# One mask operation for eight heads, and a new order of all five queues, in a fused attention and gated-MLP kernel

## The chip, the cores and the metric

The kernel runs on one core of a Trainium2 chip. The metric is the device time of one execution in microseconds (us), median of the runs shown. A core has five engines with a queue of instructions each, worked off in order: TensorE (PE: matmuls; PEld its weight loads), VectorE (DVE), ScalarE (ACT), GpSimd (POOL) and SyncE (SP), whose queue here issues nearly all DMA transfers. An engine waits for another only where an instruction waits for a semaphore.

## The reference: what is computed

One block with adaptive layer norm: sliding-window attention (16 heads of 28 columns, window 256), then a gated MLP whose gate mixes over the sequence. S = 2048, D = 448, bf16.

```python
mod = (_silu(c) @ w_mod).reshape(1, 6, 1, -1)
sa, ca, ga, sb, cb, gb = (mod[:, i] for i in range(6))
h = _layernorm(x) * (1 + ca) + sa
# attention: scores of query i and key k only where 0 <= i - k < 256
x = x + ga * (softmax(mask(q @ k.T * Dh ** -0.5)) @ v) @ wo
h = _layernorm(x) * (1 + cb) + sb
z = _gelu(h @ w_in)                       # 2048 x 1792
z1 = z[..., :896]; z2 = _layernorm(z[..., 896:])
g = w_sp @ z2 + b_sp                      # 2048 x 2048 times 2048 x 896
x = x + gb * ((z1 * g) @ w_out)
```

## The kernel before, in words

Work is listed once, as a graph: each call of `Sched.add` makes an `Op` with its possible engines, its dependencies, and the buffer slots that it takes. `Sched.order` (L155) does not plan anything. It reads a string, `PLAN`, written out by hand or by a program, of which each word is one operation: a letter for the engine (p TensorE, a ScalarE, d VectorE, t GpSimd, s SyncE), the operation's number, and the slots of its buffers. So the plan decides the engine (where an operation has a choice), the order in each queue, and the buffers; semaphore waits follow from these.

The stages, by the names that the profile shows:

- Loads. SP issues x in blocks (`load_x0` L408 for the first two pairs of tiles, `load_x` L398 for 512 rows each), w_mod and w_qkv in pieces (`load4` L404, some of them on ACT), `wv` and `wo` and the rest of w_mod (`wmodB`) through `load2` (L393), and `w_in` in three rows of 128 partitions and two halves (L432, L434). Transposed copies (`turn`, L465) go through SP as well: `hT<-xn` turns a normed tile, `hT<-o_sb` an attention output, `wspA` and `wspB` the 2048 x 2048 mixing matrix.
- First norm, per 128-row tile: statistics on VectorE (`stats`, L628, L630), a power on POOL (L632), the norm itself (L643, L650, with L648 for the negated mean), then for all but the first four tiles a transpose by DMA and a modulation of `hT` (L731).
- Queries, keys and values (TensorE L762, L796, L820, L840), evicted by ScalarE or VectorE (L771 and L772, L832 and L833, L844 and L845). L593 makes the two gates from `wmodB`, evicted as `gg_sb` (L596); L535 makes the second modulation from it.
- Attention, a loop over 16 query tiles `j` and two halves of 8 heads. A tile sees three key blocks: the far one and the near one are partly masked, the middle one is whole. Because the window's far edge and near edge together fill exactly one block, the two partly masked blocks are folded into one: L955 makes scores of a half into four PSUM banks of 512 columns, ScalarE takes the exponential of all 2048 columns at once into `PW` (L911), and VectorE multiplies the folded edges with a 0/1 mask into `PT` (L974), one operation for each of the two pairs `k` of key and query groups, 1024 columns each. L966 adds a leftover of the middle block. L1002 multiplies the probabilities with the values (`Vaug`, which also sums each row); it takes the edges from `PT` and the middle from `PW`. L1016 and L1018 normalise, SP turns the result, L1028 multiplies with wo, L1032 adds it to x.
- Second norm (same lines as the first, with the turn into `hT`), modulation L1053; then z2 (L1122, evicted with gelu by L1129, normed by L1134), z1 (L1143, L1151), the mixing product (L1167, 448 matmuls of 512 columns), its bias (L1171), the gate (L1174), the output product (L1186), the sum with x (L1196) and the store (L1201).

Where each edge lies in a bank is set by three numbers for even and odd tiles: `at_m0` and `at_hm` for the parts of the middle block, `at_f` for the two folded edges. A head's columns in `PW` take `PWT` = 576.

Of the kernel before, what the change touches and what calls it, by code (L numbers as in the profile page):

```python
# [12 lines left out]
d24 d22 p50.1 p59.3 p51.2 p58.0 p60.1 p62.0 a0 a3 a5 a7 a9 d23 d25 d26 d27 p40.1 p68.2 p74.3 p64.1 p52.0 p67.2  # L13
p53.3 p76.0 p49.3 p70.0 s1 s2 s4 d113 s6 s10 s8 a41 p45.0 p46 p47.1 p48 p73.2 p75.1 p63.2 t30 t31 t32 t35 t36
t33 d111 d114 t34 d112 t115 t37 a103 t29 t105 t38 d117.3 d116.2 p125.7 d86 d85 p128.0 p78.0 a129 a130 d106
d126 d127 d120 d121 d118 d119 a107 p83.1 p80.0 p81.1 p79.2 p77.0 p55.3 p72.2 p71.0 s12 d183 d181 p65.1 t104
p54.0 p149.1 p84.2 p140.5 p141 p150 a151 p82.1 p57.2 a142 t109 t110 t108 p137.7 p138 a139 p66.2 t122 d124.2
d123.0 p134.3 p131.6 p69.3 p56.0 p146.0 p147 p61.2 a132 d177 d184 d135 a136 s13 d243 d179 d178 d182 d180 t28
t185 t191 t187 t189 d245 d44 d241 d186.3 s11 p143.7 p370.0 a133 p164.1 p171.6 p172 d244 p165 d166 a148 p152.0
p144 d145 d173 d247 p153 d154 a371.0 p376.0 p155.1 p156 d157 a42 a377.4 p394.0 a395.1 a396 a170 t39 d380 d372  # L20
d246 d167 d374 p158.7 p159 a160 s15 p93.1 p94 d95 d248 d87 d88 d242 d397 p96.0 p97 d98 d378 s193 t188.1 s194
t190.2 s195 t192.0 s196 d197 d200 p401.0 a402.5 p174.1 p175 a176 p161.7 p162 p373.0 p89.0 p90 d91 d198 d92
a403 a43 p421.0 a422.6.0 t249 t253 d404 t251 t199 p375 p379 p381 d406 d382 d399 t252.2 d163 p217.0 p218 a219
a169 p210.1 p211 d212 p429.0 a430.0 p201.0 p202 a203 d168 p204.1 p205 a206 s14 d309 d383.2 p398.0 p400 p448.0
a449.2.1 s16 d426 s831 s258 t254.1 s259 d250.0 d255 d425 d432 d311 s384 s257 t256.3 s260 t100 t99 t261 t102
t262 t264 p226.0 p423.0 a424 p207.1 p227 p405 p208 d228 d305 p407 d408 d409.1 d306 s410 d101 d310 d431 a209
d215 d453 p456.0 p229.0 a457.1 d459 d214 d458 d452 p220.1 p221 p230 a231 p427.0 p428 s833 p475.0 p433 p434
d435 p223.0 p224 d225 d312 p450.0 a222 p232.1 d436.2 s437 d213 a476.3.2 d480 p483.0 d307 p233 d234 p235.0 p236
a451 a216 p477.0 p454.0 p455 a484.0 p501.0 d485 d486 d308 s21 s17 s834 p460 p461 d462 d479 d463.0 s464 a237
t263 p385.0 p386 d387 p411.1 p412 a478 p503.0 d413 t313 a502.6.0 p528.0 a504 d388 d505 d389 p481.0 p482 p487  # L30
p488 p271.0 p530.0 d489 d490.1 a529.2.1 d533 d506 d532 p272 a273 p509.0 a510.5 p268.1 p274.0 p275 d276 p269
d270 p507.0 p508 a531 p555.0 a556.3.2 p281.0 p265.1 p266 a267 d512 p282 p557.0 a558 a283 d511 p513 t317 t318.1
s323 t319 t320.2 s324 d314.0 s321 t315 t316.3 s322 t328 d279 d414 d560 p536.0 a537.1 p438.1 p439 d440 d280
p514 d515 d516.0 p287.0 p288 a289 p290.1 p291 a292 p563.0 a564.5 p238.0 p239 d278 p293.1 p534.0 p294 p535
p582.0 a240 p465.0 p466 d441 d442 d538 d415 d277 s20 s491 s830 s517 t390 d539 d391.2 t392 s393 a295 a583.4.0
d559 p540 p541 p284.1 p584.0 p285 a286 p590.0 a591.2 d566 d467 p299.0 p300 a301 d542 d543.1 p561.0 p562 d586
d565 d468 p567 p568 p608.0 t416 t327 t325 d326 d587 p518.1 p335.0 p519 d569 d570.0 p588.0 a585 p589 p336 d593
d469 d520 a609.3.1 p616.0 d592 d521 d417 d522 t523 t470 t418.0 t524 p338.1 p339 a337 s544 p545.0 p546 s18 p594
p595 a617.5 p635.0 a636.6.2 p610.0 a611 d340 p492.1 p493 d547 p296.0 p297 a298 t471 d596 d597.2 d612 p614.0
d613 s835 s571 s598 d494 t419 s420 d640 d548 d619 d549 d618 d495 t443 t444 t445.1 t446 s447 p662.0 a663.0.0  # L40
d667 p615 p332.0 p333 a334 p329.1 p330 a331 d639 d343 t472.2 d473 s474 p643.0 a644.1 p599.0 p600 p637.0 a638
p345.1 p346 p620 a347 d601 d602 d344 d645 d666 d342 p670.0 a671.2 p621 p664.0 d622 d496 p348.0 p349 a350
p357.1 p358 t550 t551 t552.0 t804 d623.2 s624 p689.0 d646 d673 d525.2 p302.0 p303 d304 d672 s19 p641.0 p642
p647 p648 d649 d805 t553 d650.0 s651 t526 s527 t497 t806 t803 d498.1 t499 s500 a690.5.1 p697.0 a359 p351.1
p352 d341 d353 a665 d693 d603 a698.1 d700 d694 p668.0 p363.0 p364 a365 p715.0 a716.3.2 p669 p674 p675 p691.0
a692 d699 d676 d677.2 s678 p354.1 p355 p572.0 a356 d720 d719 p723.0 a724.2 p717.0 a718 p573 d574 d575 p695.0
p696 p701 d725 p702 d703 d704.0 s705 s554 d576 p652.0 p742.0 a743.0.1 p366.1 p367 a368 d726 p653 d654 t577
d578 t579.2 d746 d655 p721.0 p722 p727 p750.0 a751.4 p728 d747 d729 d730.1 s731 p360.1 p361 p625.0 p744.0 p626
p769.0 d752 d627 d753 d628 a362 p748.0 p679.1 p680 d681 a745 p749 p754 p755 d756 d757.2 p771.0 a770.6.0 p777.0
a772 p706.1 p707 p732.0 p733 d773 d774 p775.0 p776 t580 s581 t809 a778.1 p852.0 p853.1 p854 d656 d708 d734  # L50
d779 d682 d780 d808 t604 d605.0 s758 p759.0 p760 d761 p781 p782 d783 d784.0 a856 d629 t630 t631 p855 a862
p868.3 p869.2 p870 p871 a878 a872 p980.0 p981.1 p982 p983 a986 a987 d735 d736 t657 t658 t606 t659.2 d857 d683
t810 t807 p884.3 p885.2 p886 p887 d709 d710 d632.1 d762 d763 d879 d633 s369 s825 s785 s826 s607 t684 d685 s634
a984 a985 p900.0 p901.1 p902 p903 t737 t711 t660 d686.0 t687 a894 d895 d896 t764 a888 p996.3 p997.2 p998 p999
s661 d712.1 d858 d738 s688 s840 s824 s823 a904 p988.0 d905 a814 a910 p989.1 p990 a1000 a1001 a1003 a992 a1002
a993 p786.0 t799 t797 t713 t811 t813 t801 t812 d765 d889 t766.0 d859 d863 d874 d906 s714 d864 t767 s768 d907
t739.2 d897 d912 t898 d865 d880 d890 p787 d788 d740 s741 s832 p991 a995 d789 d790 t791 d873 d911 d875 t792
d793.1 p932.2 a994 p933.0 p934 p935 a936 d937 p916.1 p917.3 a942 d944 d938 d943 d913 p918 a920 d922 p919 a926
p1004.0 p1005.1 p1006 p1007 a1011 a1009 a1010 a1008 t860 t794 s795 t818 d817 t816 d891 d815 d881 d939 d927
d899 d928 d945 t914 t876 d877 d921 t908 d909 t882 d923 p948.2 p949.3 p950 p951 p964.1 p965.0 p966 a952 d929  # L60
d953 d954 a958 d959 d955 d883 d960 t892 t956 d893 t940 p967 a968 a974 p1028.3 p1029.1 p1030 p1031 t866 t930
t946 t924 t800 a1032 a1033 p1012.2 p1013.3 p1014 a1034 p1020.0 a1035 p1021.1 p1022 p1015 a1017 a1016 a1018
a1025 p1023 a1026 a1027 a1019 a1024 d976 d961 d970 d975 d969 d977 d931 d971 t978 d861 d915 d925 d941 d947 d979
d867 s828 s822 s827 s829 s820 s844 s821 s851 s845 s850 t972 d973 d957 t962 d963 p1087.4 p1051.5 s819 p1036.1
d1037.1 d1088.0 t1038 p1048.2 p1090.4 t1089 p1042.7 d1043.0 t1044 d1049.0 t1050 p1081.3 d1082.0 t1083 s839
s836 s838 s849 s841 s843 s846 s837 s847 s842 s848 p1123.7 p1072.2 d1124.0 d1052.1 t1053 t802 t796 t1125
p1120.0 d1121.1 t1122 p1084.7 d1085.1 t1086 p1156.3 d1157.1 t1158 d1073.1 t1074 d1091.1 p1078.6 p1138.7
d1079.0 t1080 t1092 p1045.4 p1039.6 d1046.1 p1153.1 t798 t1047 d1040.0 t1041 d1139.0 p1075.6 p1114.2 p1054.4
p1141.0 p1150.7 d1055.1 t1056 d1076.1 p1060.4 p1147.6 t1077 p1096.5 t1140 d1154.0 p1144.1 d1061.3 d1115.1
p1093.2 d1097.0 t1155 d1145.0 p1102.3 p1063.1 p1057.4 t1146 d1142.0 s1098 d1103.0 t1116 p1105.5 s1062 d1151.1  # L70
d1094.3 t1152 d1058.2 s1059 d1148.1 t1149 d1106.1 t1107 p1069.4 d1070.1 s1071 d1064.1 s1095 s1065 p1108.7
p1117.5 p1111.0 d1109.1 t1110 d1112.1 t1143 p1167.2 p1066.1 t1113 p1163.4 d1118.0 t1119 s1104 d1067.0 s1068
p1168 d1169.0 s1170 p1171.0 p1172 d1173.2 s1174 p1126.3 p1129.6 d1130.0 d1127.1 s1128 s1131 p1159.5 p1160
p1164 d1161.3 s1162 p1099.2 d1165.0 d1100.2 s1101 s1166 p1132.5 d1133.3 s1134 p1135.3 d1136.1 s1137
"""


class Hold:


    def __init__(self, res):
        self.res = res
        self.slot = None
# [167 lines left out]
def bass_adaLN_cond__sliding_block__mixer_gmlp__prompt_kernel(  # L251
# [25 lines left out]
    PWT = 576  # L277
# [33 lines left out]
    mask01, _, _ = alloc("mask01", [128, 2, 128], BF16)  # L311
# [231 lines left out]
    for n in range(4):  # L543
        v, kp = n // 2, n % 2
# [116 lines left out]
    def lock_d(*a):  # L661
        op = dve(*a)
        op.lock = 2
        return op
# [604 lines left out]
```

## Time and profile before

| | us |
|---|---|
| runs shown | 277.11, 276.43, 281.8; median 277.11 |
| profiled execution | 277.96 |
| its span, first to last instruction | 276.2 |
| PE busy (modelled) / PEld busy | 268.5 / 155.1 |
| DVE / ACT / POOL busy | 163.7 / 121.5 / 118.1 |
| mask L974, 56 operations | 38.0 |

An engine's busy time is a sum over stages with different limits: attention fills about the first 110 us, z2 and z1 lead over to the mixing product, which runs alone on TensorE from 155 us on. Lines are numbers of the kernel before. A group's row gives its line, engine, operation, output and inputs with their shapes, how often it ran, its busy time in us and the mean ns of one, and after the second bar the engine's idle time just before it and what ended most of it. A row in order of time starts with its start and its length in us. A row of DMA issues gives the size of each and the median time from issue to landing.

### The profile page before, as it was taken

The page shows a single profiled execution, that of the slowest core. Times are in us where ns is not written, and L with a number is a line of the kernel's source. Part 1 is how long each engine was busy: PE and PEld are TensorE (multiplying, and loading weights), DVE is VectorE, ACT ScalarE, POOL GpSimd, SP SyncE. Part 2 cuts the span into 40 slices and gives each one's busy share as a digit, 9 for nine tenths or more (in the row PEclk, how much of TensorE's full clock was granted, in tenths as well). Part 3 has the DMA queues.
Part 4 walks back from the last instruction along what each step waited for, and adds up shares of the span by engine and source line. Part 5 has one row for each costly group of instructions (what it writes and reads, how often), then busy time and mean ns, then how long its engine had stood idle before and what let it go on. Part 6 is the DMA issues. An engine that isn't in the chain of part 4 may idle for free.

```text
span 276.2 us, 8403 instructions
## 1 busy us (share of the span) xinstructions
PE 268.5 (97%) x3751; PEld 155.1 (56%) x3751; DVE 163.7 (59%) x365; ACT 121.5 (44%) x142; POOL 118.1 (43%) x160
## 2 busy tenths in 40 slices
PE   7999998999999899999999999999999999999995
PEld 5976686678677676544444444444444444454552
DVE  3799999979899989939789301221212022153143
ACT  2599998899899689476766500000000000000000
POOL 7565467626574231498258003254453023062320
PEclk9999999999999799999999999999999999999999
DMA  7999744845442533658499996000000000001013
GB/s 206 316 221 189 96 101 114 107 96 110 114 63 61 107 60 61 176 114 141 97 155 191 213 182 135 0 0 0 2 0 0 0 2 0 33 17 63 0 39 116
DMA packets 67301, 25.54 MB, mean 92 GB/s; under 512 B 58497, under 2 KB 66178, under 8 KB 67266
## 3 DMA queue, kind: packets, MB, share of 16 engines
q1 hardware_dynamic: 66304, 24.21, 43.8%
q10 hardware_dynamic: 962, 0.80, 1.1%
q8 instruction: 29, 0.48, 0.8%
q14 instruction: 6, 0.05, 0.1%
HBM read 9.01 MB, written 1.84 MB: 39 GB/s over the span
## 4 chain that ended last, share of the span: by engine, by line
PE 78%; DVE 13%; DMA 4%; POOL 1%; SPq 1%; issue 1%; DVEq 0%
PE ps L1167 35%; PE ps L1122 8%; PE ps L1143 8%; PE ps L1186 8%; PE ps L1002 5%; DVE PT L974 4%; PE ps L1028 4%; PE ps L955 3%; DMA x_sb<-in_A_x_dram 3%; PE ps L820 3%; PE ps L762 2%; DVE st_all L628 2%; PE ps L840 2%; DMA hT<-xn 2%; DVE o_sb L1018 1%
## 5 line engine op out<-in xcount | busy, mean ns | idle before, releaser
L1174 POOL TENSOR_TENSOR z1T<-tmpg,z1T 128x512 bf16<-128x512 bf16 x28 | 32.0, 1153 | 77.2 <-DVE tmpg L1171 77.2
L1171 DVE TENSOR_TENSOR tmpg<-ps,bsp_bc 128x512 bf16<-128x512 f32 x28 | 19.0, 689 | 76.0 <-PE ps L1167 64.7
L911 ACT ACTIVATE PW<-ps 128x2048 bf16<-128x2048 f32 (+1 forms) x42 | 59.9, 1451 | 6.1 <-PE ps L955 4.5
L1167 PE MATMUL ps<-wspB,z 128*128 128x512 bf16 x224 | 50.1, 379 | 0.0
L1167 PE MATMUL ps<-wspA,z 128*128 128x512 bf16 x224 | 49.5, 379 | 0.0
L632 POOL TENSOR_TENSOR rs_all<-mv_all,neghalf 128x1 f32<-128x1 f32 (+2 forms) x37 | 24.1, 672 | 34.3 <-DVE mv_all L630 34.3
L974 DVE TENSOR_TENSOR PT<-PW,mask 128x1024 bf16<-128x1024 bf16 x56 | 38.0, 702 | 0.2
L1167 PEld LDWEIGHTS ps<-wspA,z 128*128 128x128 bf16 x224 | 21.8, 98 | 26.6 <-issue 0.4
L1167 PEld LDWEIGHTS ps<-wspB,z 128*128 128x128 bf16 x224 | 21.9, 98 | 26.2
L1002 PE MATMUL ps<-Vaug,PT 128*128 128x32 bf16 x496 | 23.3, 177 | 1.4 <-DVE o_sb L1018 1.4
L1002 PEld LDWEIGHTS ps<-Vaug,PT 128*128 128x128 bf16 x496 | 21.4, 96 | 4.3 <-DVE o_sb L1018 2.2
L1122 PE MATMUL ps<-w_in,hT 64*128 64x448 bf16 x224 | 22.0, 350 | 0.0
L1186 PE MATMUL ps<-w_out_g,z1T 128*128 128x448 bf16 (+2 forms) x119 | 22.0, 342 | 0.0
L1143 PE MATMUL ps<-hT,w_in 64*128 64x512 bf16 x196 | 22.0, 376 | 0.0
L628 DVE BATCH_NORM_STATS2 st_all<-z 128x6 f32<-128x448 bf16 x32 | 18.4, 606 | 5.8 <-ACT z L1129 5.8
L628 DVE BATCH_NORM_STATS2 st_all<-x_sb 128x6 f32<-128x448 bf16 x32 | 19.4, 615 | 2.9 <-DMA x_sb<-in_A_x_dram 2.7
L1002 PE MATMUL ps<-Vaug,PW 128*128 128x32 bf16 x224 | 19.7, 177 | 0.0
L820 PE MATMUL ps<-hT,WQK 112*128 112x128 bf16 x256 | 17.9, 223 | 1.6 <-DVE KT L833 1.1
L1151 ACT ACTIVATE z1T<-ps 128x512 bf16<-128x512 f32 x28 | 14.6, 603 | 9.1 <-PE ps L1143 9.1
L1196 DVE TENSOR_TENSOR fin<-ps,x_sb 128x448 bf16<-128x448 f32 (+2 forms) x17 | 9.8, 595 | 14.7 <-PE ps L1186 9.9
L1002 PEld LDWEIGHTS ps<-Vaug,PW 128*128 128x128 bf16 x224 | 17.6, 96 | 1.1
L1129 ACT ACTIVATE z<-ps 128x896 bf16<-128x896 f32 x16 | 13.9, 913 | 7.9 <-PE ps L1122 5.4
(105 smaller groups left out, 354.1 us busy)
## 6 DMA issues: line engine op xcount, KB each, us to landing
out_dram<-fin SPq DMA_DIRECT2D x15, 112.0 KB, 1.7
wmodB<-in_w_mod_dram SPq DMA_DIRECT2D x1, 1568.0 KB, 15.0
x_sb<-in_A_x_dram SPq DMA_DIRECT2D x3, 448.0 KB, 8.0
w_in<-in_B_w_in_dram SPq DMA_DIRECT2D x3, 448.0 KB, 4.5
w_out_g<-in_B_w_out_dram SPq DMA_DIRECT2D x1, 784.0 KB, 4.7
bsp_bc<-in_B_b_sp_dram SPq DMA_DIRECT2D x1, 512.0 KB, 5.1
x_sb<-in_A_x_dram SPq DMA_DIRECT2D x2, 224.0 KB, 4.8
hT<-xn SPq DMA_TRANSPOSE x28, 3.2
```

The costliest lines, as they stand in the source:

```text
L628: st = [dve(0.62, lambda e, t=t, o=12 - 6 * (n - ci), s=s: e.bn_stats(st_all[:, slot, t, o:o + 6], s()), deps(t), prio) for ci, s in enume ...
L632: return pool(0.4 + 0.15 * len(tiles), lambda e: e.tensor_tensor(rs_all[:, slot, a:b], mv_all[:, slot, a:b, 1], neghalf[:, 0:b - a], ALU.pow),
L820: km = lambda g, kc, start, stop, h=h, t=t: lambda e: e.matmul(ps[:, h.slot[0], g * 128:(g + 1) * 128], lhsT=WQK[0:CP, kc, 16 + 4 * g:20 + ...
L911: ex = act(xdur, lambda e, out_ap=out_ap, in_ap=in_ap: e.activation(out_ap(), in_ap(), ACT.Exp, scale=SCALE), [s] + list(after), v - 8.0 + ...
L974: return lock_d(0.68, lambda e: e.tensor_tensor(cols(hp.slot[0] * 2048 + 1024 * k, [[256, 4], [128, 2], [1, 128]]), cols(at_w() + pad + at ...
L1002: fns.append(lambda e, hp=hp, hO=hO, hi=hi, bi=bi, kb=kb, hd=hd, nb=nb, a=at[hi][bi], p_of=p_of: e.matmul(ps[:, hO.slot[0], 32 * hd:32 * h ...
L1122: return lambda e, kc, p0, start, stop: e.matmul(ps[:, hs[t % 2].slot[hf], 0:D], lhsT=hT[p0:p0 + 64, kc, t * 128:(t + 1) * 128], rhs=w_in[ ...
L1143: return lambda e, kc, p0, start, stop: e.matmul(ps[:, hs[b // 2].slot[b % 2], :], lhsT=w_in[p0:p0 + 64, kc, ft * 128:(ft + 1) * 128], rhs ...
L1167: m = pe(16 * MMS, [lambda e, h=h, si=si, ft=ft, tb=tb: e.matmul(ps[:, h.slot[0], :], lhsT=z2[:, si, ft * 128:(ft + 1) * 128], rhs=(wspA i ...
L1171: a = dve(0.7, lambda e, h=h, ht=ht, tb=tb: e.tensor_tensor(tmpg[:, ht.slot[0], :], ps[:, h.slot[0], :], bsp_bc[:, tb * 512:(tb + 1) * 512 ...
L1174: u = pool(1.16, lambda e, ht=ht, ft=ft, tb=tb: e.tensor_tensor(z1T[tb][:, ft, :], tmpg[:, ht.slot[0], :], z1T[tb][:, ft, :], ALU.mult), [ ...
L1186: return [lambda e, ft=ft: e.matmul(ps[:, h.slot[0], 0:hi - lo], lhsT=z1T[t // 4][:, ft, (t % 4) * 128:(t % 4 + 1) * 128], rhs=w_out_g[:, ...
```

## The change

Two edits. In the first, the folded edges of both pairs are put at one column step: `at_f` is now 288 columns apart, half of `PWT`, in both kinds of tiles, and `at_m0` moves into the room between. Eight edges of a half then stand 288 columns apart through all four banks, and one operation of 2048 columns masks them all. `PT` holds them in the order head, pair instead of pair, head, and L1002 reads them there. Both pairs' products with the values now depend on the one operation.

```diff
-                at_m0, at_f, at_hm = ((0, (128, 288), 448), (384, (64, 224), 0))[j % 2]
+                at_m0, at_f, at_hm = ((160, (0, 288), 448), (224, (64, 352), 0))[j % 2]
...
-                def mask_all(k, hp=hp, at_w=at_w, pad=pad, at_f=at_f):
-                    return lock_d(0.68, lambda e: e.tensor_tensor(
-                        cols(hp.slot[0] * 2048 + 1024 * k, [[256, 4], [128, 2], [1, 128]]), cols(at_w() + pad + at_f[k], [[PWT, 4], [32, 2], [1, 128]], PW),
-                        cols(0, [[0, 4], [128, 2], [1, 128]], mask01[:].rearrange("p b q -> p (b q)")), ALU.mult), [exs[0]] + t_mask, v - 7.0 + k)
-                mks = [mask_all(k) for k in range(2)]
+                mk2 = lock_d(1.2, lambda e, hp=hp, at_w=at_w, pad=pad, at_f=at_f, cols=cols: e.tensor_tensor(
+                    cols(hp.slot[0] * 2048, [[256, 8], [128, 2], [1, 128]]), cols(at_w() + pad + at_f[0], [[PWT // 2, 8], [32, 2], [1, 128]], PW),
+                    cols(0, [[0, 8], [128, 2], [1, 128]], mask01[:].rearrange("p b q -> p (b q)")), ALU.mult), [exs[0]] + t_mask, v - 7.0)
+                mks = [mk2, mk2]
...
-                    at = [[(0, 1024 * k + 256 * hi), (1, PWT * hi + at_m), (0, 1024 * k + 256 * hi + 128)] for hi in range(4)]
+                    at = [[(0, 512 * hi + 256 * k), (1, PWT * hi + at_m), (0, 512 * hi + 256 * k + 128)] for hi in range(4)]
```

The second edit replaces the whole `PLAN`. The number of operations falls from 1175 to 1147, by the 28 masks. TensorE's order of attention and MLP stays close to the old one. VectorE has 348 operations instead of 365, POOL 144 instead of 156, ScalarE one more: some evictions, norms and small copies change engines. The largest moves are at the front. SP's queue begins, before and after (one row is one transfer; sizes from the profile before):

```
before                               after
x, tiles 0 and 1         224 KB      w_in, a row of 128       448 KB
w_mod, sa part           196 KB      x, tiles 0 and 1         224 KB
w_mod, ca part           196 KB      w_mod, sa part           196 KB
w_qkv, keys              196 KB      w_in, a row of 128       448 KB
x, tiles 2 and 3         224 KB      wo                       392 KB
w_qkv, queries           196 KB      w_mod, ca part           196 KB
x, second block          448 KB      w_qkv, keys              196 KB
x, third block           448 KB      w_in, a half             224 KB
wv                       392 KB      x, tiles 2 and 3         224 KB
wmodB                   1568 KB      w_qkv, queries           196 KB
hT<-xn, 4 transposes                 w_in, a row of 128       448 KB
x, fourth block          448 KB      x, second, third, fourth 448 KB each
wo                       392 KB      wv                       392 KB
                                     hT<-xn, 1 transpose
                                     wmodB                   1568 KB
                                     hT<-xn, 3 transposes
```

On ACT, the silu of c, which waits for a small matmul, now stands ahead of the four loads of w_mod and w_qkv that ACT issues; before, it stood behind them. On VectorE, the statistics of x's fourth block come among the first forty operations. On TensorE, the filler matmuls that need no data are spread over the early steps in another way.

More of the change, by code (lines that the diff above doesn't have):

```diff
@@ L18 @@
[L18 to L22, printed above, removed]
@@ L75 @@
+s1073 t1079 s1070 p1140 p1131.7 p1132 p1143.5 p1101.6 p1135.0 p1136 d1033.1 d1141.0 d1102.3 p1098.6 p1144
+s1034 s1142 d1133.0 d1137.1 p1104.4 s1103 s1134 p1107.0 d1099.2 d1145.3 d1105.0 s1138 d1108.1 s1106 s1100
+s1146 s1109
 """
```

115 lines of the change are left out of this document (58 added, 57 removed).

## The prediction

> **What bounds the kernel now.** I read the page's slices first, then the chain that ended last, then the early DMA queue, because the change alters all three.
>
> ```profile
> span 276.2 us, 8403 instructions
> ...
> PE   7999998999999899999999999999999999999995
> ...
> DVE  3799999979899989939789301221212022153143
> ...
> PEclk9999999999999799999999999999999999999999
> DMA  7999744845442533658499996000000000001013
> ...
> PE 78%; DVE 13%; DMA 4%; POOL 1%; SPq 1%; issue 1%; DVEq 0%
> ```
>
> Each digit is a fortieth of the span, 6.9 us. TensorE looks full everywhere, but its busy time is modelled; VectorE is full from 14 to some 110 us, and the DMA engines are full in the first 28 us, where all weights and x arrive. The chain in order of time says where a microsecond counts:
>
> ```profile
> 3.91 7.49 DMA x_sb<-in_A_x_dram
> ...
> 21.05 4.35 DMA hT<-xn
> ...
> 155.13 76.08 PE ps L1167 x352
> ...
> 260.74 12.41 PE ps L1186 x70
> 273.18 0.62 DVE fin L1196
> ```
>
> It begins with a transfer: the second block of x is issued at 3.91 us and lands at 11.40. It ends in a long stretch in which TensorE alone sets the pace. So a delay at the front reaches the end unless some wait between them shrinks. The stretches by engine show what could shrink:
>
> ```profile
> core 0: us, PE busy (x) PEld busy (x) DVE busy (x) ACT busy (x) POOL busy (x), PEclk, DMA share, GB/s
> 10.00:12.00 2.00, 1.94 (x34) 1.95 (x35) 1.75 (x6) 0.58 (x1) 1.54 (x4) 1.00 1.09 379
> 12.00:18.00 6.00, 6.00 (x94) 5.09 (x92) 5.52 (x18) 5.72 (x9) 2.71 (x8) 1.00 1.06 286
> 22.40:111.10 88.70, 85.86 (x2484) 62.59 (x2484) 83.33 (x180) 78.87 (x79) 43.71 (x53) 0.98 0.53 98
> 111.10:131.00 19.90, 19.90 (x212) 9.74 (x209) 15.29 (x41) 11.66 (x18) 14.59 (x26) 1.00 0.68 146
> 84.00:98.00 14.00, 12.61 (x380) 9.98 (x378) 12.96 (x27) 10.52 (x11) 4.39 (x7) 0.88 0.41 86
> ```
>
> In the attention stage VectorE works 83.33 of 88.70 us, so it is idle for 5.4 us; after 111 us TensorE has no gap. VectorE's idle time is thus most of what a late start can be made up from.
>
> **Part one, the mask.** Two operations of 1024 columns become one of 2048, 28 times.
>
> ```profile
> L974 DVE TENSOR_TENSOR PT<-PW,mask 128x1024 bf16<-128x1024 bf16 x56 | 38.0, 702 | 0.2
> ...
> L1002 PE MATMUL ps<-Vaug,PT 128*128 128x32 bf16 x496 | 23.3, 177 | 1.4 <-DVE o_sb L1018 1.4
> ...
> L628 DVE BATCH_NORM_STATS2 st_all<-x_sb 128x6 f32<-128x448 bf16 x32 | 19.4, 615 | 2.9 <-DMA x_sb<-in_A_x_dram 2.7
> ...
> L995 DVE TENSOR_TENSOR PT<-PT,mask 128x512 bf16<-128x512 bf16 x8 | 3.0, 399 | 0.0
> ...
> L833 DVE CAST KT<-ps 128x512 bf16<-128x512 f32 x3 | 2.0, 658 | 0.0
> L650 DVE TENSOR_SCALAR xn<-x_sb,rs_all,nm_all 128x448 bf16<-128x448 bf16 x4 | 1.9, 470 | 0.0
> ...
> L648 DVE TENSOR_SCALAR nm_all<-mv_all,rs_all 128x1 f32<-128x1 f32 x6 | 1.2, 203 | 0.5 <-POOL rs_all L632 0.5
> ```
>
> 512 columns take 399 ns and 1024 take 702, so 512 more cost 303 ns and 96 ns is fixed. One mask of 2048 is then 702 + 2 x 303 = 1308 ns against 2 x 702 = 1404: 28 x 96 ns = 2.7 us of VectorE saved. Bounds: nothing, if the long one costs twice the short, and 28 x (702 - 303) = 11.2 us, if the second half cost only a 512-column slope; the fit through two sizes stands nearer, so I take 2.7. The Trainium skill, VectorE: DVE Perf Modes, section "The perf-mode tier table", gives 1224 ns for a bf16 tensor_tensor of 2048 columns; by it the saving would be 28 x 180 ns = 5.0 us, and no row here has that size.
>
> The first pair of heads now waits for the whole mask, 0.6 us more. That is free as long as TensorE has other work queued, and it has: the only producer behind L1002's idle time in its row is o_sb, never the mask. Without that cover it would be at most 28 x 0.6 = 17 us.
>
> **Part two, who does what.** The plan also moves evictions and copies between engines. Between the first gg eviction and the last mask VectorE goes from 180 operations to 158: 28 mask operations go away net, and of the rest it gains four key evictions (L833, 4 x 658 ns = 2.6 us), three norms (L650, 1.4), four negated means (L648, 0.8) and seven more evictions, norms and copies of about 0.4 us each (2.8); it loses three statistics (L628, 1.8), which stand ahead of that point now, and nine small copies and aggregates of about 0.28 us (2.5). That is 7.6 - 4.3 = 3.3 us more. Less the 2.7 of the mask, the stretch carries the same VectorE work, +0.6 us: the mask's gain is spent.
>
> **Part three, the front of SP's queue.** This decides. SP issued x, w_mod, w_qkv and x again first:
>
> ```profile
> 0.79 0.46 SPq L408 DMA_DIRECT2D x_sb<-in_A_x_dram  x1
> ...
> 3.91 1.20 SPq L398 DMA_DIRECT2D x_sb<-in_A_x_dram  x2
> 5.15 1.01 SPq L393 DMA_DIRECT2D wv<-in_A_wqkv_dram  x1
> 6.20 2.23 SPq L393 DMA_DIRECT2D wmodB<-in_w_mod_dram  x1
> 17.10 6.13 SPq L465 DMA_TRANSPOSE hT<-xn  x4
> ```
>
> ```profile
> wmodB<-in_w_mod_dram SPq DMA_DIRECT2D x1, 1568.0 KB, 15.0
> x_sb<-in_A_x_dram SPq DMA_DIRECT2D x3, 448.0 KB, 8.0
> w_in<-in_B_w_in_dram SPq DMA_DIRECT2D x3, 448.0 KB, 4.5
> ...
> w_in<-in_B_w_in_dram SPq DMA_DIRECT2D x2, 224.0 KB, 3.8
> ...
> wv<-in_A_wqkv_dram SPq DMA_DIRECT2D x1, 392.0 KB, 9.2
> wo_g<-in_A_wo_dram SPq DMA_DIRECT2D x1, 392.0 KB, 5.7
> ```
>
> The last column is the time from issue to landing. A block of 448 KB takes 4.5 us in a quiet stretch (w_in) but 8.0 at the front (x), and each load of the front lands behind those issued before it: the queue is served in order, at 286 to 379 GB/s with the engines at a share above 1. The new order puts three whole w_in blocks, one half block and wo, none of which the attention stage's start needs, ahead of the second block of x: 3 x 448 + 224 + 392 = 1960 KB, 2.01 MB. At 379 GB/s that is 5.3 us, at 286 it is 7.0; I take 6.4. So x's second block lands at 11.4 + 6.4 = 17.8 us. Behind it the third and fourth blocks of x come, then wv, which TensorE's queue needs before most of its early work: 448 KB more, 2.47 MB in all and 8.1 us, so about 22.5 instead of 14.4.
>
> Then the wmodB load. It was issued at 6.20, ahead of every transpose. In the new order it stands behind the first transpose of xn, and that waits in SP for the norm of tile 4, which needs the second block of x. Before, x landed at 11.4 and that transpose was issued at 17.1, 5.7 us later (four statistics, the power on POOL, the norm). The new queue has the same work there: 17.8 + 5.7 = 23.5, and 1.2 for the transpose's own issue gives 24.7 for wmodB. Its 1.6 MB at 286 GB/s take 5.6 us, and a quiet w_in block shows 4.5 - 1.6 = 2.9 us beside its bytes, so it lands near 33, against 6.2 + 15.0 = 21.2. With the bounds of the rate and without any fixed part it would be 30; so the load is 9 to 12 us late, and I take 11.
>
> What waits for it is TensorE's L593, and all of TensorE's queue behind it, and the eviction of gg on VectorE:
>
> ```profile
> 11.42 1.15 DVE L628 BATCH_NORM_STATS2 st_all<-x_sb 128x6 f32<-128x448 bf16 x2 [0.18 <-DMA x_sb<-in_A_x_dram]
> ...
> 21.43 1.67 PE L593 MATMUL ps<-wmodB,sc_rep 112*128 112x448 bf16 x8
> ...
> 22.41 0.60 DVE L596 COPY gg_sb<-ps 128x448 f32<-128x448 f32 x1
> ...
> 111.59 0.67 DVE L974 TENSOR_TENSOR PT<-PW,mask 128x1024 bf16<-128x1024 bf16 x1
> ```
>
> L593 moves from 21.4 to about 32.4, gg's eviction from 22.4 to 33.4. VectorE's work ahead of that eviction hides inside the wait. The early statistics of x's last block are done there too, which part two has counted. ACT's four early loads move behind the silu; they share the full engines, the bytes ahead of x stay the same, so I price that at nothing, and at up to 2 us if they held w_mod's columns back further, time that the wait for wmodB covers.
>
> **The sum.** From gg's eviction to the last mask before: 22.4 to 112.3 us. The same work at the same density ends 11 + 0.6 us later. Some of the 5.4 us of VectorE's idle time should go, since w_in and wo are already there and their transfers no longer sit between the transposes; but most of these gaps come from engines that all shift together, so I take back 2.6, about half. After the last mask TensorE has no slack, and the order of L1122, L1143 and L1167 costs the same: +9.0 us at the end. The profiled execution took 277.96 us with a span of 276.2, 1.8 outside it; 276.2 + 9.0 + 1.8 = 287.0. That execution lies 0.85 above the median of 277.11, so against the runs I predict 286.1, say 286.
>
> **Rivals.**
> Absorbed on the way: all of VectorE's idle time, and the wait at its lower bound, 9 us. For it: TensorE's one named wait in L1002 is VectorE's o_sb, so room on VectorE would help it too. Against: the idle time is spread over many small waits. 277.1 + 9 + 0.6 - 5.4 = 281.3, and 279 with a mask saving of 5 instead of 2.7, between its bounds.
>
> The front doesn't matter (the other side): w_in's big rows ride beside x, so that x lands by 13 us. It decides at that point: with x late by under 2 us the transpose and wmodB are issued by 20 and hidden behind statistics. For it: the 379 GB/s stretch shows that the engines can carry more than 286. Against: their share is above 1 in both stretches. Then the mask's 2.7 us and the loads gone from the middle remain: 277.1 - 2.7 - 1 = 273.4, and down to 271 if the gap of TensorE at 84 to 98 closes too.
>
> The clock: the row of 84 to 98 us shows 0.88 granted after TensorE stood idle for 1.4 us, its only slow stretch; (1 - 0.88) x 14 = 1.7 us. TensorE, out of work before wmodB lands, would stand idle for 4 us or more near 28, and for some 2 near 20, so two such stretches could cost 3.4 us: 286.1 + 3.4 = 289.5. The Trainium skill, TensorE: Matmul & The Clock Gate, section "What's actually happening", has the clock at half after an idle window of about 3.4 us and until a busy one; by that rule the wait near 28 us would trigger it.
>
> The long mask runs slower than the fit: at worst as bad as two, which is +2.7 us on VectorE, inside the forecast's own range.
>
> **How the numbers follow.** Forecast (282.6 to 289) 0.68; absorbed (279 to 282.6) 0.10; clock on top (289 and more) 0.11; the front doesn't matter 0.11, half of it under 271.6. A measurement of this kernel tells about 2%, 5.5 us: slower from 282.6 up. Slower 0.68 + 0.11 = 0.79, same 0.10 + 0.05 = 0.15, faster 0.06. The range takes the forecast, the absorbed case and the start of the clock case: 279 to 290.5; for slower alone 282.6 to 290.5.
>
> **What would show it.** Right: the first wait of VectorE for x's second block ends near 17.8; wmodB is issued after 22 and lands after 30; L593 starts after 30; masks of 1.2 to 1.35 us; from gg's eviction to the last mask 86 to 91 us; the first L1167 near 164. Wrong: x's second block before 13 us, or wmodB issued before 18, would fell part three; a last mask before 116 in spite of a late wmodB would mean that the stage had more slack than VectorE's idle time shows.

## The result and the profile after

The new kernel takes 296.12 us (median of four, 295.08 to 298.09) against 277.11 for the kernel before (median of three, 276.43 to 278.88). A further run of the kernel before, at 281.80 us, was a slow one and is left out. The ratio of the means is 1.068, with a 95% interval of 1.058 to 1.078. That is slower, as forecast, but by 18.9 us (by the means) where the forecast had 9. The profiled execution is the longest of the four, 298.09 us with a span of 296.4, so its rows show 20.2 us more than the 276.2 of before. In the new kernel lines stand one to four lower (L1167 of before is L1163, L974 is L971); in the experiments up to eight lower.

The page of the new kernel, span, slices and shares of the chain:

```profile
span 296.4 us, 8376 instructions
...
PE   5589389898999999999999999999999999999995
...
DVE  2157639997899999997779931131111023221244
...
PEclk9999869999999999999999999999999999999999
DMA  7991948387463312489769996000000000200003
...
PE 72%; DVE 15%; DMA 9%; issue 1%; SPq 1%; ACT 1%; POOL 0%; DVEq 0%
```

TensorE's first slices are emptier than before, the granted clock falls to 0.8 and 0.6 in slices 5 and 6 (some 30 to 44 us), and DMA's share of the chain has gone from 4% to 9%. The chain that ended last, in order of time, start and length:

```profile
3.18 12.56 DMA wmodA<-in_w_mod_dram
15.78 1.74 PE ps L544 x16
...
26.90 1.02 POOL rs_all L631
...
29.73 8.48 DMA wmodB<-in_w_mod_dram
38.26 2.42 PE ps L592 x6
...
175.20 10.74 PE ps L1163 x49
```

Two marks divide the loss of this execution. The wmodB matmuls start at 38.26 instead of 21.43, 16.8 us late. From there to the first L1163 it takes 175.20 - 38.26 = 136.9 us, against 155.13 - 21.43 = 133.7 before: 3.2 us more. From that L1163 to the end it takes 121.2 us, against 121.1 before: nothing more is lost there. So five sixths of the loss is made in the first 38 us.

The chain doesn't begin with x, as it did before, but with the first columns of w_mod, which are multiplied with the silu of c (L544; L545 before) to shift and scale every normed tile. The load that it follows is SP's own second load of w_mod, issued at 3.18 instead of 1.81, behind two rows of w_in and wo. Rows in order of time, with the idle time before each and what ended it, of the kernel before and then of the new one:

```profile
1.35 0.88 ACTq L404 DMA_DIRECT2D wmodA<-in_w_mod_dram  x2
...
5.20 1.49 PE L545 MATMUL ps<-sc_sb,wmodA 112*112 112x112 bf16 x16
6.91 1.03 PE L545 MATMUL ps<-sc_sb,wmodA 112*112 112x112 bf16 x16 [0.21 <-DMA wmodA<-in_w_mod_dram]
```

```profile
1.33 1.28 ACT L517 ACT_TABLE_LOAD   x1 [1.33 <-PEq L1250]
2.65 0.91 ACTq L403 DMA_DIRECT2D wmodA<-in_w_mod_dram  x2
...
15.78 1.74 PE L544 MATMUL ps<-sc_sb,wmodA 112*112 112x112 bf16 x16 [1.88 <-DMA wmodA<-in_w_mod_dram]
...
21.02 0.63 DVE L627 BATCH_NORM_STATS2 st_all<-x_sb 128x6 f32<-128x448 bf16 x1 [0.16 <-DMA x_sb<-in_A_x_dram]
...
28.38 1.30 SPq L464 DMA_TRANSPOSE hT<-xn  x1
29.73 0.57 SPq L392 DMA_DIRECT2D wmodB<-in_w_mod_dram  x1
...
40.71 0.62 DVE L595 COPY gg_sb<-ps 128x448 f32<-128x448 f32 x1 [6.48 <-PE ps L592]
```

The last of w_mod's first columns reaches TensorE at 15.78, where before it came at 6.91. x's second block lands at 21.0 instead of 11.4. The first transpose, wmodB behind it, and gg's eviction follow.

The granted clock around the wait (start and end, then busy time and count of PE, PEld, DVE, ACT and POOL; clock, DMA share, GB/s):

```profile
32.00:36.00 4.00, 0.35 (x7) 0.17 (x4) 2.23 (x9) 2.30 (x4) 0.00 (x0) 0.87 1.01 306
36.00:38.20 2.20, 0.00 (x0) 0.00 (x0) 0.00 (x0) 0.00 (x0) 0.00 (x0) 0.50 1.25 196
38.26:40.00 1.74, 1.74 (x5) 0.73 (x6) 0.00 (x0) 0.00 (x0) 1.74 (x3) 0.50 1.13 251
40.00:42.00 2.00, 2.00 (x26) 0.78 (x25) 0.96 (x2) 0.73 (x1) 0.42 (x1) 0.55 0.00 0
42.00:44.00 2.00, 2.00 (x53) 1.63 (x49) 1.54 (x6) 1.97 (x4) 0.72 (x1) 1.00 0.00 0
...
38.26:131.20 92.94, 88.98 (x2492) 62.09 (x2494) 84.30 (x158) 78.39 (x74) 39.96 (x52) 0.98 0.49 80
```

While TensorE waits for wmodB its clock falls to half, and it stays there until 42. The six matmuls of L592 take 2.42 us, 0.40 each, where the eight of before took 1.67, 0.21 each. The attention stage as a whole holds 84.30 us of VectorE's work, against 83.33 before. The shares of the clock date the fall: 0.87 over the four us from 32 means full speed until about 35.0, some 2.6 us after TensorE ran dry at 32.35.

### The profile page after: what moved, and what is told of

Same layout as the page of the kernel before. It is cut to its first block, busy times and chain, and to the rows that moved or that the text cites. A ratio compares the mean times of both kernels' runs of the same rounds, so it can differ in the third digit from the quotient of the medians.

```text
span 296.4 us, 8376 instructions
## 1 busy us (share of the span) xinstructions
PE 273.9 (92%) x3741; PEld 156.4 (53%) x3751; DVE 165.9 (56%) x348; ACT 124.5 (42%) x143; POOL 110.8 (37%) x148
## 4 chain that ended last, share of the span: by engine, by line
PE 72%; DVE 15%; DMA 9%; issue 1%; SPq 1%; ACT 1%; POOL 0%; DVEq 0%
PE ps L1163 32%; PE ps L1139 7%; PE ps L1182 7%; PE ps L1118 6%; DVE PT L971 5%; DMA wmodA<-in_w_mod_dram 4%; PE ps L998 3%; DMA wmodB<-in_w_mod_dram 3%; PE ps L761 3%; PE ps L954 2%; PE ps L1024 2%; PE ps L819 2%; DVE st_all L627 1%; PE ps L839 1%; DMA hT<-o_sb 1%; DVE o_sb L1014 1%
## 5 line engine op out<-in xcount | busy, mean ns | idle before, releaser
L1167 DVE TENSOR_TENSOR tmpg<-ps,bsp_bc 128x512 bf16<-128x512 f32 x28 | 19.2, 690 | 77.9 <-PE ps L1163 76.6
L1163 PE MATMUL ps<-wspB,z 128*128 128x512 bf16 x218 | 48.5, 379 | 0.3
L1163 PE MATMUL ps<-wspA,z 128*128 128x512 bf16 x220 | 48.5, 379 | 0.3 <-issue 0.2
L631 POOL TENSOR_TENSOR rs_all<-mv_all,neghalf 128x1 f32<-128x1 f32 (+2 forms) x37 | 25.4, 698 | 49.5 <-DVE mv_all L629 44.7
L971 DVE TENSOR_TENSOR PT<-PW,mask 128x2048 bf16<-128x2048 bf16 x28 | 35.7, 1282 | 0.4 <-ACT PW L910 0.2
L1163 PEld LDWEIGHTS ps<-wspA,z 128*128 128x128 bf16 x224 | 21.8, 98 | 26.6 <-issue 0.4
L1163 PEld LDWEIGHTS ps<-wspB,z 128*128 128x128 bf16 x224 | 21.9, 98 | 26.3
L998 PE MATMUL ps<-Vaug,PT 128*128 128x32 bf16 x496 | 25.1, 177 | 1.5 <-DVE o_sb L1014 0.9
L998 PEld LDWEIGHTS ps<-Vaug,PT 128*128 128x128 bf16 x496 | 22.6, 96 | 6.0 <-DVE o_sb L1014 1.2
L1118 PE MATMUL ps<-w_in,hT 64*128 64x448 bf16 x224 | 22.7, 349 | 0.0
L1139 PE MATMUL ps<-hT,w_in 64*128 64x512 bf16 x196 | 22.6, 376 | 0.0
L998 PE MATMUL ps<-Vaug,PW 128*128 128x32 bf16 x224 | 20.8, 176 | 0.0
L998 PEld LDWEIGHTS ps<-Vaug,PW 128*128 128x128 bf16 x224 | 17.8, 96 | 2.0
L819 PE MATMUL ps<-hT,WQK 112*128 112x128 bf16 x256 | 17.8, 222 | 0.0
L954 PEld LDWEIGHTS ps<-qT,KT 32*128 32x128 bf16 (+1 forms) x1344 | 13.4, 90 | 7.8 <-ACT PW L910 5.2
L1192 DVE TENSOR_TENSOR fin<-ps,x_sb 128x448 bf16<-128x448 f32 (+2 forms) x17 | 9.8, 593 | 13.7 <-PE ps L1182 11.9
```

What stands on the lines that cost most here:

```text
L631: return pool(0.4 + 0.15 * len(tiles), lambda e: e.tensor_tensor(rs_all[:, slot, a:b], mv_all[:, slot, a:b, 1], neghalf[:, 0:b - a], ALU.pow),
L819: km = lambda g, kc, start, stop, h=h, t=t: lambda e: e.matmul(ps[:, h.slot[0], g * 128:(g + 1) * 128], lhsT=WQK[0:CP, kc, 16 + 4 * g:20 + ...
L954: fm.append(lambda e, hm=hm, qi=qi, key=key, kn=kn, lo=lo, hi=hi, col=col, p0=p0, t=t, j=j: e.matmul(ps[p0:p0 + kn, hm.slot[t], col:col + ...
L971: mk2 = lock_d(1.2, lambda e, hp=hp, at_w=at_w, pad=pad, at_f=at_f, cols=cols: e.tensor_tensor(cols(hp.slot[0] * 2048, [[256, 8], [128, 2] ...
L998: fns.append(lambda e, hp=hp, hO=hO, hi=hi, bi=bi, kb=kb, hd=hd, nb=nb, a=at[hi][bi], p_of=p_of: e.matmul(ps[:, hO.slot[0], 32 * hd:32 * h ...
L1118: return lambda e, kc, p0, start, stop: e.matmul(ps[:, hs[t % 2].slot[hf], 0:D], lhsT=hT[p0:p0 + 64, kc, t * 128:(t + 1) * 128], rhs=w_in[ ...
```

## The experiments

A word of PLAN is one operation; the words that matter: s18, s17, s19 are the w_in rows, s21 the half, s16 wo, s15 wmodB, s193 to s196 the first four transposes, a41 the silu, a3 and a5 ScalarE's two loads of w_mod, a7 and a9 its two of w_qkv. Only the order in a queue is edited unless said. Times stand against the kernel before of the same batch; where two changed kernels are compared, the difference of their ratios to it is taken, times 277.5 us, the mean of the kernel before in the result.

**Undoing the front of SP's queue in the new kernel: the loads, wmodB, both.**

```diff
# late_w                          # wmod_early
-t36 d24 s18 p57.2                -s193 ... s15
+t36 d24 p57.2                    +s15 s193 ...
 ... (s17, s16, s21, s19 too)
 s196
+s18 s17 s16 s21 s19
```

> The new kernel with only the five early loads of w_in and wo moved in SP's queue from the front to behind the four transposes of the first xn; the wmodB load stays behind the first transpose. Theory F (the front decides, all of the loss comes from late x and late wmodB): x's second block lands near 12 instead of 21.0, the first transpose is issued near 19 instead of 28.4, wmodB lands near 28 instead of 38.3, and the time falls by 10 us to about 286. Rival R (the new order behind the front, with its moved evictions and the long mask, is what costs): the front moves the same but the attention stage gives it back, and the time stays above 292.

> The new kernel with only the wmodB load moved in SP's queue, to just ahead of the first transpose of xn (behind wv); w_in and wo stay in front. Theory F: x's second block stays late (21.0) but wmodB is issued near 17.6 and lands near 29 instead of 38.3; VectorE and TensorE are then bound by x being 9.6 us late, and the time falls by 8 us to about 288. Rival R: above 292. Rival T (wmodB is hidden, late x alone decides): no change, 296.

> The new kernel with both moves: w_in and wo behind the first transposes, wmodB ahead of them, that is SP's front nearly as in the kernel before, all else new. Theory F: x's second block lands near 12, wmodB near 22, and the time is 276 to 280, no slower than before by more than 1%. Rival R: 285 or more. Rival A (TensorE's fillers and ScalarE's early loads, which stay in the new order, carry a part): 281 to 285.

Measured: 290.01, 291.12 and 284.45 us, with 277.99 before, ratios of 1.045, 1.048 and 1.024; that is 6.4, 5.5 and 12.3 us less than the new kernel. The two moves add (6.4 + 5.5 = 11.9). Each brings less than Theory F said. With late loads TensorE still waits until 9.13 for columns of w_mod, which ScalarE issues behind its silu, the first transpose comes at 23.2 and the wmodB matmuls start at 33.1. With an early wmodB they start at 32.3, since x and w_mod are then late; with both moves, at 24.3. With both, 6.5 us are left (ratio 1.024, 1.017 to 1.030), in the range named for ScalarE's early loads or TensorE's fillers: SP's front is most, not all.

**The same front in the kernel before, whole and in two halves.**

```diff
 s1
+... s18 first; s17 s16 behind s2; s21 behind s6; s19 behind s8      (loads; front)
-s15 s193 s194
+s193 s15 s194                                                       (wmod_late; front)
+s14 behind s13                                                      (front)
```

> The kernel before with only SP's front made as in the new kernel: w_in's three blocks, its half block and wo ahead of x's second block, x's fourth block ahead of wv, and wmodB behind the first transpose; all other queues and the two short masks are the old ones. Theory F: wmodB lands near 38, and the time rises by 17 to 19 us to about 296. Rival R: it rises by 8 at most, to 286, since the old order behind the front takes the rest back.

> The kernel before with only the wmodB load moved behind the first transpose of xn; w_in and wo stay late. Theory Q (wmodB's landing sets the start of the attention stage, and nothing later takes a delay back): it is issued near 18.3, takes 8.8 us as in the kernel with the whole front, lands near 27 instead of 21.2, and the time rises by 5 to 6.5 us to about 284. Rival K (the stage takes half of it back, as the prediction assumed): 280 to 281.

> The kernel before with only w_in's four loads and wo moved to the front of SP's queue, wmodB still ahead of the first transpose. Theory Q: x's second block lands near 17.8 and wmodB near 27.5, 6.4 us late, and the time rises by 6 to 8 us to about 285; together with the wmodB move alone that makes the 14.6 of both. Rival K: 281 to 282. If the two alone make much less than 14.6, they are worse together than apart.

Measured: the whole front 292.62 us (ratio 1.053, 1.047 to 1.059), 14.6 more, where Theory F had 17 to 19; wmodB late alone 286.22 against 278.18, 8.0 more, above the 5 to 6.5 of Theory Q; the loads alone 285.12, 6.9 more, as it said. 8.0 + 6.9 = 14.9: again they add. The chains of the three, the whole front first (with VectorE's first wait for x's second block, in order of time, behind it):

```profile
3.31 8.77 DMA wmodA<-in_w_mod_dram
12.12 1.75 PE ps L541 x16
...
25.52 8.80 DMA wmodB<-in_w_mod_dram
34.37 3.17 PE ps L589 x8
...
169.96 76.08 PE ps L1163 x352
```

```profile
17.84 1.15 DVE L624 BATCH_NORM_STATS2 st_all<-x_sb 128x6 f32<-128x448 bf16 x2 [0.44 <-DMA x_sb<-in_A_x_dram]
```

```profile
19.44 8.79 DMA wmodB<-in_w_mod_dram
28.28 3.17 PE ps L589 x8
...
162.48 10.74 PE ps L1163 x49
```

```profile
3.46 10.09 DMA wmodA<-in_w_mod_dram
...
29.49 4.49 DMA hT<-xn
...
162.87 10.74 PE ps L1163 x49
```

With the whole front, x's second block lands at 17.84, which is the forecast's 17.8, and wmodB is issued at 25.52 (forecast 24.7). But the chain runs through w_mod's columns, which reach TensorE at 12.12, then through TensorE's own queue up to 24.7; x isn't on it. From the wmodB matmuls to the first L1163: 135.6 with the whole front, 134.2 with wmodB late, against 133.7 before. Next to nothing of the delay is taken back. In the first two the eight wmodB matmuls take 3.17 us instead of 1.67, which is the halved clock. With the loads alone wmodB isn't on the chain; the delay is that of w_mod's columns and the transposes. Its wmodB matmuls start at 29.86, 8.4 us late, and L1163 at 162.87, 7.7 us late: 0.7 us come back, of 8.4. (In this profile the clock was at half from about 8 to 18 us, in and behind the waits for w_mod's columns.)

**ScalarE's silu.**

```diff
# silu             # silu_mid           # silu_back, a_front
-a3 a5 a7 a9 a41   -a3 a5 a7 a9 a41     -a41 a3 a5 a7 a9
+a41 a3 a5 a7 a9   +a3 a5 a41 a7 a9     +a3 a5 a7 a9 a41
```

> The kernel before with only ScalarE's silu moved ahead of its four early loads. Theory S: the loads are issued 1.3 us later, x's second block lands 1 to 2 us later, and the time rises by 2 to 3 us to 280 or 281. Rival B: within 1 us of 278, since the bytes ahead of x stay the same.

> The kernel before with the silu between ScalarE's two loads of w_mod's columns and its two of w_qkv, instead of behind all four. Theory C (what costs is that SP's later loads get ahead of w_mod's columns): these land as before, near 5 and 7, and the time stays within 1 us of 277.5. Rival T (the activation-table load of 1.28 us ahead of a load, or any late load of ScalarE's, costs by itself): 279 to 281.

> The kernel before with SP's front as in the new kernel and ScalarE's silu ahead of its four loads; all behind it, and the two short masks, as before. Theory Q (the first instructions of the two DMA-issuing queues make the whole loss): the two edits add, 14.6 + 4.7 = 19.3, and the time is 295 to 298, as with the new kernel. Rival O (the new order behind the front makes a part of it, and the two edits overlap): 291 to 294.

> The new kernel with only the silu put back behind ScalarE's four loads, SP's front left as it is. Theory Q: 3 to 4.7 us less, 291.5 to 293; x's second block lands near 18 instead of 21.0. Rival H (the wait for wmodB covers the late columns of w_mod, as the prediction held): within 1.5 us of 296.

> The new kernel with both moves of SP's queue (w_in and wo late, wmodB early) and, besides, ScalarE's silu put back behind its four early loads. Theory S (the silu holds these loads back by 1.3 us, and that is what is left of the late front): the first L592-type matmul on wmodB starts under 1 us late instead of 3.4, and the time falls by 3 us to about 281.5. Rival B (TensorE's fillers between the early steps and VectorE's new order do it): no change, 284 to 285.

Measured: the silu first in the kernel before, 281.63 against 276.94, 4.7 more (ratio 1.014, 1.009 to 1.020), above the 2 to 3 of Theory S. In the middle, 277.94 against 278.14, no change (0.997 to 1.004): it isn't the table load, nor a late load as such, but w_mod's columns. On top of the late front the silu adds 1.6 (294.92, just under the 295 of Theory Q); taking it back in the new kernel gives 2.4 (294.68, nearer to rival H, that the wait for wmodB covers it, than to Theory Q); in the undone front it gives 0.6 (282.69, where 281.5 was expected). In each of these three the intervals of the two kernels overlap. So alone it costs 4.7, and behind another delay about half of that or less, which these runs can't tell from zero. The columns come no later for it there: TensorE's last wait for them ends at 12.09 with front and silu, at 12.12 with the front alone. Rows of the kernel with the silu first, and below them what each DMA queue carried from 4 to 8 us (q1 is SP's, q10 ScalarE's; packets, MB, share), in the kernel before and with the silu first:

```profile
3.07 0.85 ACTq L400 DMA_DIRECT2D wmodA<-in_w_mod_dram  x2
...
9.29 2.49 PE L541 MATMUL ps<-sc_sb,wmodA 112*112 112x112 bf16 x24 [3.48 <-DMA wmodA<-in_w_mod_dram]
```

```profile
q10 hardware_dynamic: 707, 0.59, 55.6%
q1 hardware_dynamic: 727, 0.61, 52.4%
```

```profile
q1 hardware_dynamic: 772, 0.65, 64.0%
q10 hardware_dynamic: 307, 0.26, 24.7%
```

Before, both queues have work and move the same, 0.59 and 0.61 MB. Issued 1.7 us later, ScalarE's two loads of w_mod move 0.26 MB in that stretch, and TensorE is through with the columns at 9.29 + 2.49 = 11.8 instead of 6.91 + 1.03 = 7.9. The Trainium skill, DMA: Bandwidth & Descriptors, section "Queues, rings and completion order", says that each DMA engine takes packets in turn from the queues that have work; the even split agrees. The bytes ahead of x stay the same, as the prediction had it; what changes is which load gets the shares.

**The mask alone, both ways.** In the kernel before, the two masks become the one of the new kernel, in the second one's place; in the kernel with the undone front, the one is issued as two:

```diff
-                mk2 = lock_d(1.2, lambda e, ...: e.tensor_tensor(<2048 columns>), ...)
+                def both(e, ...):
+                    for k in range(2):
+                        last = e.tensor_tensor(<1024 columns, from 2 * PWT * k on>)
+                    return last
+                mk2 = lock_d(1.2, both, ...)
```

> The kernel before with only the mask edit: one mask of 2048 columns for eight heads, standing where the second of the two stood, the order of all five queues otherwise the old one. Theory V: 28 x 0.12 = 3.4 us less on VectorE, and the time falls by 2 to 3.4 us to about 275. Rival W (the first pair of heads waits for the whole mask and TensorE runs dry): 278 or up to 2 us more.

> The same kernel with each long mask issued as two of 1024 columns, back to back in the same place. By the profile of the new kernel the long one takes 1.28 us on average and two short ones 1.40: 28 x 0.12 = 3.4 us more on VectorE. Theory V (VectorE sets the pace of the attention stage): 2 to 3.4 us slower than with the long mask. Rival H (VectorE has room): within 1 us of it.

Measured: 276.98 against 276.94 (ratio 0.9997, 0.996 to 1.003), and 282.55 against 282.69 with the long mask. No effect either way. The group's row in the new kernel, in the kernel before with the long mask, and in the new one with two:

```profile
L971 DVE TENSOR_TENSOR PT<-PW,mask 128x2048 bf16<-128x2048 bf16 x28 | 35.7, 1282 | 0.4 <-ACT PW L910 0.2
```

```profile
L967 DVE TENSOR_TENSOR PT<-PW,mask 128x2048 bf16<-128x2048 bf16 x28 | 34.7, 1249 | 0.1
```

```profile
L969 DVE TENSOR_TENSOR PT<-PW,mask 128x1024 bf16<-128x1024 bf16 x56 | 38.1, 724 | 0.1
```

VectorE does save, 38.0 - 34.7 = 3.3 us of busy time in the kernel before, 38.1 - 35.7 = 2.4 in the new one. The end doesn't move. In the first test the longer wait of the first pair of heads (rival W) could hide a gain, but its profile shows 0.3 us of waits for the mask in all; in the second both pairs wait for the whole mask either way. So work of this size on VectorE, 94% busy in this stage, doesn't set its length; a full engine is not yet the bound. Nor is an operation's share of the chain its price: the masks have 4% of the chain of before, 12 us.

**What the new order costs behind an undone front.** With SP's and ScalarE's fronts as before, 5.7 us are left (282.69 against 276.94, ratio 1.021), although the wmodB matmuls start at 21.94, only 0.5 late. Four attempts to find them:

```diff
# front_norms: the third group's norms and transposes up
 t254.1
+d251 d250.0 d252.2 s260 s258 s257 s259
# front_xn: the same, and the w_in loads from behind s196 to behind s259
# sp_loads: wo right behind s196, w_in between later transposes as before
# sp_loads2: the same, and two w_sp loads (s802, s804) as late as before
```

> The new kernel with the old front of both queues and, besides, the norms of the third group of four tiles moved up to where their inputs are ready, their four transposes ahead of the w_sp loads, and w_in's loads behind them. Theory N (the new order costs what it does in the attention stage because this group's transposes come 8 to 18 us later than before, which TensorE's projections then wait for): 2 to 4 us less than the 282.7 of the kernel without this move. Rival E (the moved evictions and copies cost it): within 1 us of 282.7.

> The new kernel with the old front of both queues, and only the norms of the third group of tiles and its four transposes moved up; w_in's loads stay right behind the first transposes, so that they cannot collide with the transposes of o_sb as in the kernel with both moves. Theory N (these late transposes cost the new order its 5.7 us): 278 to 281. Rival E (something else in the order costs it): 282 or more.

> The new kernel with the old front of both queues, and wo issued right behind the first transposes, with w_in's blocks between the later transposes as in the kernel before, instead of all five right behind the first transposes, where wo landed at 32.0 behind w_in and stood on the chain that ended last. Theory P (the 5.7 us left to the new order are the place that the earlier test gave these loads, not the order of the other queues): 277 to 280. Rival E (the order of the other queues costs them): 282 or more.

> The same, and two of the w_sp loads, which the new order issues ahead of the third group's transposes, moved back to where the kernel before has them. Theory W2 (these two loads hold up the transposes behind them): 1 to 3 us less than the same kernel without this move. Rival E: within 1 us of it.

Measured: 289.92, 284.79, 283.33 and 283.65 us, against 278.14, 278.18 and, for the last two, 278.37. The first is 6 us worse, and tells nothing of the norms: the loads of w_in and three transposes of the mixing matrix are issued only from 39 to 50 us, and the first transposes of the attention output behind them, as SP's rows show. The first output is ready at 33.1, and VectorE stands idle for 7.29 us until its transpose has landed.

```profile
39.10 1.05 SPq L427 DMA_DIRECT2D w_in<-in_B_w_in_dram  x2
40.20 2.00 SPq L429 DMA_DIRECT2D w_in<-in_B_w_in_dram  x1
...
43.39 7.15 SPq L460 DMA_TRANSPOSE wspA<-in_B_w_sp_dram  x3
50.59 2.58 SPq L460 DMA_TRANSPOSE hT<-o_sb  x2
```

The other three stand at ratios of 1.021, 1.014 and 1.018, with intervals that overlap that of the kernel without the move. So neither the late transposes of the third group nor the place of w_in, wo and two w_sp loads is shown to be the cause, and none of them is the whole of it; a part of some 2 us isn't excluded. In the kernel with the undone front wo did stand on the chain (as the expectation says), and giving it its old place brought little.

The traces do show where the new order loses. From the start of the wmodB matmuls to the first mixing matmul they take, in us, one execution of each kernel:

| order behind the front | clock full at the start | clock at half at the start |
|---|---|---|
| old | 131.4 to 133.7, five kernels | 134.2 to 135.6, three kernels |
| new | 135.3 to 137.7, seven kernels | 136.9 to 137.6, three kernels |

(The kernel with w_in's loads in the way, 142.5, is left out.) By the middle kernel of each group the new order takes 4.6 us longer with the clock at full (137.3 against 132.7) and 2.3 with it at half (137.1 against 134.8). So it costs time on this stretch in the new kernel too, 136.9 us against 134.8 with the two fronts in the old order. With the undone front it is lost ahead of the first matmul of z2, 91.96 us behind the wmodB matmuls instead of 88.66, and TensorE stands idle for 4.67 us of that instead of 2.84. Which moved operation makes it is open. By the times, 294.92 for the two fronts in the old order leaves 2.6 us for the new order in the new kernel (ratios of 1.059 and 1.068), which the intervals alone can't tell from zero.

## Why the direction was right and the size was not

By the ratios, the 18.9 us are: SP's front 14.8, the silu 1.6 on top of it, the rest of the new order 2.6 (each rounded). The forecast's 9 were 11 for SP's front, 0 for the silu, 0.6 for VectorE's work, less 2.6 taken back. The difference, term by term:

| step | forecast | shown | by |
|---|---|---|---|
| wmodB matmuls late by SP's front | 11 | 12.9 | 34.37 - 21.43, the front alone |
| from there to L1163 | -2.6 | +1.9 | 135.6 - 133.7, the front alone, one execution each; of it 3.17 - 1.67 = 1.5 by the halved clock |
| silu | 0, up to 2 | 1.6, not to be told from zero | ratios 1.0588 - 1.0532 |
| all else | 0.6 | 2.6 by the ratios, some 2 in the traces | 1.0681 - 1.0588; 136.9 - 134.8 |

**Taking back 2.6 us** is the step that failed most. VectorE's 5.4 us of idle time aren't a reserve: in the old order, a late start with the clock at full left the stretch at 132.4 and 133.0 us, and without a delay it took 131.4 to 133.7. From gg's eviction to the end of the last mask the new kernel took 91.3 us, just outside the 86 to 91 that were named, against 89.9 before. That a delay shifts all engines together, and the gaps with them, fits this and is argued. And where the forecast had a gain stands a loss, the clock.

**The clock** was a rival with 0.11, apart from the forecast; it is a part of the case itself. The wait that the forecast worked out, "4 us or more near 28", was 5.9 us long, and the clock stayed at half until 42. By the Trainium skill, TensorE: Matmul & The Clock Gate, section "What's actually happening", an idle window of some 3.4 us halves it and a busy one of that length frees it. The freeing agrees: 38.26 to 42, 3.7 us. The halving came sooner here, 2.6 us after TensorE ran dry, and in the kernel before after a wait of 1.4 us, the only one between 84 and 98 us, which was followed by a clock of 0.50 from 92 to 95:

```profile
90.94 0.19 PE L1002 MATMUL ps<-Vaug,PT 128*128 128x32 bf16 x1 [1.39 <-DVE o_sb L1018]
```

A wait of 3.1 us early in the new kernel, up to 8.19, left the clock full. So the length of a single wait doesn't decide it in these traces, and a shorter one than the section names can be enough. The forecast had the wait and the price (3.4 us for two stretches) in hand, and left them out of its sum.

**The front of SP's queue** was the right mechanism, and its links are as forecast in the kernel with this edit alone: x's second block at 17.8, the transpose issued at 24.2 (said 23.5), 8.8 us from wmodB's issue to its landing (said 8.3). These links add up to 12.9 late, above the 9 to 12 that the forecast allowed and the 11 that it took. What it had wrong besides is the load that counts. It followed x's second block, because the chain of before begins with it. The chain of the new order begins with w_mod's first columns, for which TensorE already waited before, at 6.91; it gets them at 12.12 with the front alone and at 15.78 in the new kernel's profile, and works off its queue behind them until the norm of tile 4 can go. In that profile, x's block landed at 21.0 and the wmodB matmuls were 16.8 us late, not 12.9; that execution is 2 us above the median, and with the same order of both queues' loads in the old kernel they start at 34.65. What makes the 3.6 us between is not shown.

**The silu** cost 1.6 us behind the late front, within the bound of 2 named for it, and these runs can't tell it from the nothing of the forecast. The mechanism, w_mod's columns held back, is shown where the silu alone is first (4.7 us), and not behind the late front, where the columns come no later.

**The mask** was about right in size: two at 1.40 us became one of 1.25 to 1.28, and the estimate was 1.31. The Trainium skill's 1224 ns, from VectorE: DVE Perf Modes, section "The perf-mode tier table", lies as near, on the other side. Its worth at the end, none, came out as forecast for another reason: the forecast had other work on VectorE spend the gain, and the runs show that the gain doesn't move the end at all. **Who does what** held as a count of VectorE's work, 84.30 us against 83.33; that the order of the other queues costs time all the same, 2.3 to 4.6 us by the traces, is a term that the forecast lacked.

Of the rivals, that the front doesn't matter is excluded by the front alone, 14.6 us, and that it is absorbed on the way by the stretches from wmodB to L1163.

## What to carry to other kernels

Ahead of the first stage, put nothing in a load queue that the stage doesn't need, and move no load behind an instruction that waits on data: here 2 MB of loads ahead cost 7 us, a load behind a transpose that waits for a norm 8, and the two add. When a delay at the front is priced, list each early load with its consumer and what that waited before, rather than follow the one on the old chain; give nothing back for idle time seen later, and add the clock that a long wait costs. A nearly full engine may still not set the pace: a run in which its operation is made longer or shorter, with all else in place, shows that.

## What the runs showed of the hardware

Two loads of 196 KB, issued 1.7 us later on ScalarE's queue while SP's queue had work, left the columns that they carry finished 3.8 us later (11.8 against 7.9), and both queues together moved 0.91 MB from 4 to 8 us instead of 1.20, although no byte was added. Why the total falls as well is open.

TensorE's granted clock fell to half after a wait of 1.4 us (kernel before, ended at 90.94; 0.50 from 92 to 95) and within one of 5.9 us (new kernel, ended at 38.26; 0.50 from 36 to 40), and stayed full through one of 3.1 us (new kernel, ended at 8.19). At half, eight matmuls of 448 columns took 3.17 us instead of 1.67.
